# Attention with query/key norm, followed by a gated MLP: score matmuls in clusters of two, weights in eight gated transfers, the gains' load on another queue, and 24 head transposes instead of 14 on TensorE

## The chip, the core and the metric

The kernel runs on one core of one Trainium2 chip. The metric is device microseconds of one execution. Lower is better. A run counts as slow when it is over 1.5% above the fastest run of the same kernel. "TensorE" is PE in the profile, "VectorE" is DVE, "ScalarE" is ACT, "GpSimd" is POOL, "SyncE" is SP.

## The reference, cut to what matters

```python
# q, k, v: (8 batches, 12 heads, 448 tokens, 64), f32; x: (3584, 768); w_in: (768, 2048); w_out: (2048, 768)
q_n, k_n = rmsnorm(q, g_q), rmsnorm(k, g_k)               # over the 64 columns of a head
attn = softmax(q_n @ k_n.T / 8)                            # per head, 448 x 448
x = (attn @ v) -> transposed to (3584 tokens, 768)
h = x @ w_in
g = h * clip(h + 3, 0, 6) / 6
out = g @ w_out                                            # (3584, 768), f32
```

## The kernel before

The work is cut into 48 head pairs (8 batches of 6). A pair is loaded, squared, reduced, scaled to `qks` (bf16), transposed to `kq`, and its keys are multiplied by the product of the two gains `gp` and give `kp`. The scores of a pair come in four steps (`t`), each a matmul for each of the two heads, and each step is followed by an exponential on ScalarE. The values are then gathered, normalised and transposed into `xT`. While one batch is in the attention, the MLP of the batch before it runs between its matmuls on TensorE, with the result `gT` of the first half made by ScalarE and VectorE.

No instruction order is written by hand. Every step is put into a plan with a duration and a due time; a list scheduler on the host orders all steps, and each engine then executes its own in that order. The durations in the plan are guesses. They set an order and nothing else: in the traces below, an instruction starts when its data and its buffers are ready and its engine's earlier instructions are done.

```python
    g_load = add("POOL", 2.5, 0, load_g, xfer=0.1)         # four small loads, issued by GpSimd
    g_make = add("DVE", 0.3, 0, <gp = 8 * gq_t * gk_t>, g_load)
    # ... head pair P
        if P < NPE:                                        # NPE = 7
            # PE transposes of qks into a PSUM buffer of the ring M, then kp and kq by VectorE
        else:
            tr = add("SP", 1.3, at - 5.5, <nc.sync.dma_start_transpose(out=kq, in_=qks)>, ...)
            ks = add("DVE", 0.25, at - 1, <kp = kq[:, 0] * gp>, tr, ...)
    # ... scores
        for t in range(T):
            ps, swar, s_use = S_r.take()                   # S: two PSUM buffers
            s = add("PE", 0.25, at + step * t / T, score, *ks, *swar)     # two matmuls
            x = add("ACT", 0.85, at + step * t / T + 0.2, <e[t] = exp(ps)>, s, *war)
    # ... weights, f32 in memory, bf16 in the core, cast by the transfer
    for c in range(4):
        W_in[c] = add("POOL", 0.9, 12 + 6 * c, lambda c=c: load_w_in(c), xfer=5.3)
    for c in range(8):
        W_out[c] = add("POOL", 0.9, 36 + 3.5 * c, lambda c=c: load_w_out(c), xfer=2.7)
```

Of the kernel before, what the change touches and what calls it, by code (L numbers as in the profile page):

```python
# [20 lines left out]
class Step:  # L21


    __slots__ = ("eng", "dur", "fn", "due", "deps", "xfer", "start", "end", "n")

    def __init__(self, eng, dur, due, fn, deps, xfer=0.0):
        self.eng, self.dur, self.due, self.fn, self.xfer = eng, dur, due, fn, xfer
        self.deps = [d for d in deps if d is not None]
        self.start = self.end = None


class Plan:
# [4 lines left out]
    DMA_LATENCY = 1.7  # L37

# [3 lines left out]
    def add(self, eng, dur, due, fn, *deps, xfer=0.0):  # L42
        s = Step(eng, dur, due, fn, deps, xfer)
        s.n = len(self.steps)
        self.steps.append(s)
        return s

    def order(self):
# [9 lines left out]
        dma_free = 0.0  # L58
# [3 lines left out]
        def release(s):  # L62
            ready[id(s)] = max([0.0] + [
                d.end + (0.06 if d.eng == s.eng and not d.xfer else self.LAT[d.eng]) for d in s.deps])
            open_[s.eng].append(s)
# [5 lines left out]
        while len(done) < len(self.steps):  # L71
# [13 lines left out]
            if s.xfer:  # L85
                dma_free = max(dma_free, s.end) + s.xfer
                s.end = dma_free + self.DMA_LATENCY
# [24 lines left out]
def kernel(  # L112
# [63 lines left out]
    NPE = 7  # L176
    START, FIRST, SECOND, SLOT = 9.0, 4.1, 5.4, 7.9
# [7 lines left out]
    def load_g():  # L185
        for a in range(2):
            nc.gpsimd.dma_start(out=gq_t[a * 64:(a + 1) * 64, :], in_=g_q.rearrange("(p o) -> p o", o=1))
            nc.gpsimd.dma_start(out=gk_t[a * 64:(a + 1) * 64, :], in_=g_k.rearrange("(p o) -> p o", o=1))
# [13 lines left out]
    g_load = add("POOL", 2.5, 0, load_g, xfer=0.1)  # L202
    g_make = add("DVE", 0.3, 0, lambda: nc.vector.scalar_tensor_tensor(
# [10 lines left out]
    def load_w_out(c):  # L214
        nc.gpsimd.dma_start(
            out=w_out_sb[:, 2 * c:2 * c + 2, :],
            in_=moe_w_out[c * 256:(c + 1) * 256, :].rearrange("(f p) n -> p f n", p=128))
# [3 lines left out]
    L, V, KQ = {}, {}, {}  # L221
# [17 lines left out]
    def prep(P):  # L239
# [4 lines left out]
        early = P < 2  # L244
# [13 lines left out]
        else:  # L258
# [3 lines left out]
        red = add("DVE", 1.2, at - 8, lambda: nc.vector.tensor_reduce(  # L262
            out=ssq[0:PT], in_=sq[0:PT].rearrange("p i h (t d) -> p (i h t) d", d=D), axis=AX_X, op=ADD),
            *parts, *war)
        use.append(red)
        rs, war, rs_use = rs_r.take()

        def rstd():
            nc.scalar.activation(out=rs[0:PT], in_=ssq[0:PT], func=LN, bias=D * 1e-6)  # L269
            nc.scalar.activation(out=rs[0:PT], in_=rs[0:PT], func=EXP, scale=-0.5)  # L270

        r = add("ACT", 0.45, at - 7, rstd, red, *war)
        ssq_use.append(r)
        qks, war, qks_use = qks_r.take()
        rs4 = rs[0:PT].rearrange("p (i h t) -> p i h t", i=2, h=2)
        sc = []
        for i in range(2):
            e = "DVE" if P < 2 and i == 0 else "POOL"
            sc.append(add(e, 0.65 if e == "DVE" else 1.1, at - 6, lambda i=i, e=e: (
                nc.vector if e == "DVE" else nc.gpsimd).tensor_tensor(  # L280
                    out=qks[0:PT, i].rearrange("p t h d -> p h t d"),
                    in0=qk[0:PT, i].rearrange("p h (t d) -> p h t d", d=D),
                    in1=rs4[:, i].unsqueeze(3).to_broadcast([PT, 2, T, D]), op=MULT), r, *war))
# [6 lines left out]
        vf_use.append(vc)  # L290
        kq, war, kq_use = kq_r.take()
# [30 lines left out]
    XT, R = {}, {}  # L322

    def attend(P):
# [5 lines left out]
        for t in range(T):  # L330
            ps, swar, s_use = S_r.take()

            def score(t=t, ps=ps):
                for a in range(2):
                    rows = slice(a * 64, a * 64 + 64)
                    nc.tensor.matmul(out=ps[:, a, 0:S], lhsT=kp[rows, t * PT:t * PT + 128],  # L336
                                     rhs=kq[rows, 1, :], start=True, stop=True)

            s = add("PE", 0.25, at + step * t / T, score, *ks, *swar)
            x = add("ACT", 0.85, at + step * t / T + 0.2, lambda t=t, ps=ps: nc.scalar.activation(  # L340
                out=e[0:PT, t], in_=ps[0:PT, :, 0:S], func=EXP), s, *war)
            s_use.append(x)
            exps.append(x)
            kq_use.append(s)
            kp_use.append(s)
        at += step
# [10 lines left out]
        for s in range(NS):  # L357
            av.append(add("PE", 0.31, at + 0.15 * step * s, lambda s=s: values(
# [6 lines left out]
        rest = add("PE", 0.31, at + 0.45 * step, lambda: values(  # L365
# [98 lines left out]
    def y_group(b, i, n, due, span):  # L464
# [4 lines left out]
        for p in range(4):  # L469
            def mm(p=p):  # L470
                for f in range(4 * p, 4 * p + 4):
# [3 lines left out]
                             W_out[2 * p], W_out[2 * p + 1], *war))  # L475
# [27 lines left out]
    def mlp(hb, yb, t0, t1, lead):  # L503
# [17 lines left out]
        for kind, b, what, c in res:  # L521
            due, span = t0 + (t1 - t0) * at / total, (t1 - t0) * c / total
            at += c
            if kind == "h":
                h_group(b, what, due, span)
            else:
                y_group(b, *what, due, span)

    for c in range(4):
        W_in[c] = add("POOL", 0.9, 12 + 6 * c, lambda c=c: load_w_in(c), xfer=5.3)  # L530
    for c in range(8):
        W_out[c] = add("POOL", 0.9, 36 + 3.5 * c, lambda c=c: load_w_out(c), xfer=2.7)

    AHEAD = 5
    for P in range(AHEAD):
        loads(P)
    prep(0)
# [48 lines left out]
```

## Time and profile before

| | before |
|---|---|
| median of the first three runs | 481.65 us (480.47 to 483.04) |
| profiled run, its span | 482.57 us, 480.8 us |
| first scores on TensorE | 16.50 us |
| first w_in matmul on TensorE | 61.85 us |
| TensorE work by spacing (below) | 415.5 us |
| loss (span less that work) | 65.3 us |

The page of the kernel before opens with the span and the busy time of each engine.

```profile
span 480.8 us, 9258 instructions
PE 436.2 (91%) x3658; PEld 237.9 (49%) x3658; DVE 246.6 (51%) x429; ACT 253.3 (53%) x421; POOL 220.9 (46%) x218
```

TensorE is the only engine near its limit. The table by stretches of the kernel before shows where it is and where it isn't; its first row names the columns (start and end of the stretch in us, its length, then busy us of each engine with the number of instructions, the granted TensorE clock, the mean busy share of the DMA engines, and what they moved).

```profile
core 0: us, PE busy (x) PEld busy (x) DVE busy (x) ACT busy (x) POOL busy (x), PEclk, DMA share, GB/s
10.00:48.00 38.00, 24.07 (x220) 14.10 (x220) 21.62 (x37) 18.13 (x29) 20.83 (x23) 0.81 1.17 243
48.00:60.00 12.00, 8.07 (x89) 5.23 (x87) 5.73 (x11) 5.78 (x13) 10.56 (x11) 0.64 1.13 251
60.00:78.00 18.00, 16.72 (x128) 9.59 (x127) 10.59 (x21) 9.80 (x20) 9.37 (x9) 0.98 0.80 177
78.00:100.00 22.00, 18.81 (x196) 10.13 (x195) 14.52 (x24) 17.33 (x30) 20.68 (x17) 1.00 0.73 148
200.00:250.00 50.00, 50.00 (x430) 26.25 (x429) 29.11 (x50) 29.91 (x49) 27.15 (x24) 1.00 0.57 144
```

From 200 to 250 us TensorE is busy in all of the 50 us, so only less TensorE work can shorten that stretch. Before 60 us it is busy in two thirds of the time and at a lower clock, while the DMA share is above 1.1. A share can exceed 1 because the times of packets overlap; no stretch shown here goes above 1.17, so I read 1.1 and more as full. After 60 us the DMA is no longer full in this kernel.

A busy TensorE still hides a cost. The timeline of the kernel before, TensorE alone, has an isolated pair of score matmuls between w_in matmuls (start in us, duration, instruction, shapes, count).

```profile
250.65 0.82 PE L447 MATMUL M<-xT,w_in_sb 128*128 128x512 bf16 x3
251.40 0.36 PE L336 MATMUL S<-kq,kp 64*128 64x448 bf16 x2
251.70 0.82 PE L447 MATMUL M<-xT,w_in_sb 128*128 128x512 bf16 x3
```

Three w_in matmuls of 512 columns and the two score matmuls take 251.70 - 250.65 = 1.05 us together. The three take 0.216 us each in an unbroken sequence, which leaves 0.40 us for the score pair. Where two such pairs stand next to each other, both take 0.59 us. So a pair costs 0.196 us, and each stretch of score matmuls costs about 0.20 us more for going into and out of their shape (64 rows instead of 128). Priced in this way over the built instruction order, TensorE's work is 415.5 us. I call the time at a point less the priced work up to it the loss: it is 42.2 us at the first w_in matmul, 53.5 at 110 us, 58.2 at 159 us, 58.45 at 417 us, and 65.3 at the end.

The start of the kernel before, timeline of VectorE and TensorE (in brackets: idle time of the engine before the instruction, and what ended it):

```profile
9.23 0.16 DVE L203 SCALAR_TENSOR_TENSOR gp<-gq_t,gk_t 128x1 f32<-128x1 f32 x1 [9.23 <-DMA gk_t<-in_g_k_dram]
12.74 0.93 PE L300 MATMUL M<-ident,qks 112*128 112x112 bf16 x8 [12.74 <-DVE qks L280]
16.50 0.93 PE L336 MATMUL S<-kq,kp 64*128 64x448 bf16 x4
39.11 0.55 PE L336 MATMUL S<-kq,kp 64*128 64x448 bf16 x2
61.85 0.34 PE L447 MATMUL M<-xT,w_in_sb 128*128 128x384 bf16 x1
```

VectorE's first instruction is the product of the gains, and it waits 9.23 us for them. The first reduction stands behind it, and the first transposes of TensorE behind that. The isolated score pair at 39.11 us takes 0.55 us; the one at 251.40 above took 0.36. The first w_in matmul starts at 61.85 us. The waits of GpSimd from 15 to 60 us in the kernel before (total us, number of times, longest):

```profile
POOL w_out_sb L215 <- DMA w_in_sb<-in_moe_w_in_dram: 10.6, 3, 5.6
```

GpSimd, which also scales the heads, stands for 10.6 us because the issue of a w_out transfer waits for w_in transfers issued before it.

### The profile page before, as it was taken

To read this page: it belongs to the slowest core of one execution; us is meant where nothing else is said; L and a number is where in the kernel's file an instruction comes from. 1 tells how busy PE (TensorE), PEld (TensorE's weight loads), DVE (VectorE), ACT (ScalarE), POOL (GpSimd) and SP (SyncE) were. 2 spreads that over 40 slices of the span, in tenths; PEclk is the share of its full clock that TensorE was granted. 3 is DMA by queue.
4 is the path that set the end of the run, shared out by engine and by line. 5 is a ranking of instruction groups with operands and counts; after the bars stand their busy time and mean duration, and the time that the engine had idled before them with its cause. 6 is when DMAs were issued, how large, how long until landed. Compare 5 with 4: busy or idle time off the path is not lost.

```text
span 480.8 us, 9258 instructions
## 1 busy us (share of the span) xinstructions
PE 436.2 (91%) x3658; PEld 237.9 (49%) x3658; DVE 246.6 (51%) x429; ACT 253.3 (53%) x421; POOL 220.9 (46%) x218
## 2 busy tenths in 40 slices
PE   0667698968999999999999999999999999999996
PEld 0334454534444555555445565554545555644463
DVE  2636457565877775454566445544444343433421
ACT  3445454885567565656676466655655555322200
POOL 7834866998789853655354634652231000000000
PEclk9985699998999999999999999999999999999999
DMA  7999984999787845766458567562413312211122
GB/s 190 245 245 240 251 183 111 187 194 210 194 231 135 204 102 132 169 169 160 117 132 154 134 148 174 120 172 55 99 29 73 78 49 51 59 34 33 34 64 67
DMA packets 103531, 65.26 MB, mean 136 GB/s; under 512 B 62400, under 2 KB 100032, under 8 KB 103488
## 3 DMA queue, kind: packets, MB, share of 16 engines
q1 hardware_dynamic: 98048, 58.38, 51.5%
q0 software_dynamic: 5440, 6.29, 7.4%
q8 instruction: 28, 0.46, 0.4%
q14 instruction: 15, 0.12, 0.1%
HBM read 45.61 MB, written 11.01 MB: 118 GB/s over the span
## 4 chain that ended last, share of the span: by engine, by line
PE 71%; POOL 10%; issue 8%; DMA 6%; DVE 2%; ACT 2%; POOLq 0%; ACTq 0%
PE M L472 30%; PE M L447 25%; PE S L336 8%; PE X L351 6%; POOL qks L280 4%; DMA w_in_sb<-in_moe_w_in_dram 4%; POOL sq L259 3%; PE R L351 2%; DMA kq<-qks 2%; POOL va L288 1%; DVE gT L455 1%; ACT t L453 1%; ACT e L340 1%; DVE kp L314 1%; POOL sq L251 0%
## 5 line engine op out<-in xcount | busy, mean ns | idle before, releaser
L340 ACT ACTIVATE e<-S 112x896 bf16<-112x896 f32 x192 | 171.4, 915 | 100.6 <-PE S L336 99.3
L447 PE MATMUL M<-xT,w_in_sb 128*128 128x384 bf16 (+1 forms) x768 | 170.5, 354 | 4.4 <-DVE y L480 1.9
L472 PE MATMUL M<-w_out_sb,gT 128*128 128x384 bf16 x896 | 161.6, 326 | 0.7 <-DVE gT L455 0.3
L280 POOL TENSOR_TENSOR qks<-qk,rs 112x512 bf16<-112x512 f32 x94 | 97.6, 1057 | 94.1 <-DMA kq<-qks 60.2
L455 DVE SCALAR_TENSOR_TENSOR gT<-t,M 128x384 bf16<-128x384 f32 (+1 forms) x128 | 79.2, 619 | 82.6 <-ACT t L453 82.3
L453 ACT ACTIVATE t<-M 128x384 f32<-128x384 f32 (+1 forms) x128 | 69.5, 543 | 81.8 <-PE M L447 78.6
L472 PEld LDWEIGHTS <-gT 128*128 128x128 bf16 x896 | 81.3, 98 | 60.1 <-issue 12.6
L447 PEld LDWEIGHTS <-w_in_sb 128*128 128x128 bf16 x768 | 66.8, 97 | 70.0 <-issue 21.1
L259 POOL TENSOR_TENSOR sq<-qk 112x1024 f32<-112x1024 f32 x41 | 78.5, 1919 | 20.1 <-DMA qk<-in_q_dram 13.8
L351 PEld LDWEIGHTS <-e 112*128 112x128 bf16 x1536 | 71.3, 102 | 31.0 <-issue 10.5
L336 PE MATMUL S<-kq,kp 64*128 64x448 bf16 x384 | 71.2, 384 | 11.1 <-ACT e L340 6.4
L480 DVE COPY y<-M 128x384 f32<-128x384 f32 x56 | 31.2, 557 | 70.0 <-PE M L472 70.0
L351 PE MATMUL X<-va,e 112*128 112x65 bf16 x1152 | 61.9, 201 | 1.9 <-ACT e L340 1.5
L262 DVE TENSOR_REDUCE ssq<-sq 112x16 f32<-112x1024 f32 x48 | 58.0, 1212 | 10.5 <-POOL sq L259 10.3
L288 POOL CAST va<-vf 112x512 bf16<-112x512 f32 x48 | 30.2, 630 | 31.7 <-PE R L351 18.1
L336 PEld LDWEIGHTS <-kp 64*128 64x128 bf16 x384 | 18.2, 94 | 51.7 <-issue 41.9
L314 DVE TENSOR_SCALAR kp<-kq,gp 128x448 bf16<-128x448 bf16 x41 | 24.5, 598 | 13.5 <-PE S L336 9.9
L377 DVE TENSOR_TENSOR xn<-X,rd 128x384 bf16<-128x384 f32 x48 | 26.8, 558 | 1.6
L300 PE MATMUL M<-ident,qks 112*128 112x112 bf16 x56 | 6.9, 284 | 21.5 <-DVE qks L280 14.7
L376 DVE RECIPROCAL rd<-X 128x6 f32<-128x6 f32 x48 | 9.3, 194 | 29.1 <-PE X L351 29.0
L351 PE MATMUL R<-va,e 112*128 112x65 bf16 x384 | 21.7, 201 | 0.0
L269 ACT ACTIVATE rs<-ssq 112x16 f32<-112x16 f32 x48 | 10.4, 216 | 12.7 <-POOL qks L280 6.7
(27 smaller groups left out, 69.3 us busy)
## 6 DMA issues: line engine op xcount, KB each, us to landing
qk<-in_k_dram SPq DMA_DIRECT2D x48, 224.0 KB, 3.6
qk<-in_q_dram SPq DMA_DIRECT2D x48, 224.0 KB, 3.9
vf<-in_v_dram SPq DMA_DIRECT2D x48, 224.0 KB, 3.8
w_in_sb<-in_moe_w_in_dram POOLq DMA_DIRECT2D x4, 768.0 KB, 22.1
w_out_sb<-in_moe_w_out_dram POOLq DMA_DIRECT2D x8, 384.0 KB, 28.5
out_dram<-y SPq DMA_DIRECT2D x8, 336.0 KB, 3.2
out_dram<-y SPq DMA_DIRECT2D x8, 288.0 KB, 2.7
out_dram<-y SPq DMA_DIRECT2D x8, 240.0 KB, 2.8
```

Source lines behind the costliest of these rows:

```text
L259: parts.append(add("POOL", 1.95, at - 12, lambda: nc.gpsimd.tensor_tensor(out=sq[0:PT], in0=qk[0:PT], in1=qk[0:PT], op=MULT), *ld, *war))
L262: red = add("DVE", 1.2, at - 8, lambda: nc.vector.tensor_reduce(out=ssq[0:PT], in_=sq[0:PT].rearrange("p i h (t d) -> p (i h t) d", d=D), ...
L280: nc.vector if e == "DVE" else nc.gpsimd).tensor_tensor(
L288: vc = add("POOL", 0.7, at - 3, lambda: nc.gpsimd.tensor_copy(out=va[0:PT, :, :, 0:D], in_=vf[0:PT].rearrange("p h (t d) -> p h t d", d=D) ...
L336: nc.tensor.matmul(out=ps[:, a, 0:S], lhsT=kp[rows, t * PT:t * PT + 128], rhs=kq[rows, 1, :], start=True, stop=True)
L340: x = add("ACT", 0.85, at + step * t / T + 0.2, lambda t=t, ps=ps: nc.scalar.activation(out=e[0:PT, t], in_=ps[0:PT, :, 0:S], func=EXP), s ...
L351: nc.tensor.matmul(out=dst[:, a * E1:(a + 1) * E1], lhsT=e[0:PT, t, a, c0:c0 + 128], rhs=va[0:PT, a, t, :], start=(first and a == 0 and t ...
L447: nc.tensor.matmul(out=m[:, 0:n], lhsT=w_in_sb[:, kt, f * 128:(f + 1) * 128], rhs=X[:, kt, :], start=(kt == 0), stop=(kt == NKT - 1))
L453: r = add("ACT", 0.08 + n / 1200, due + span, lambda: nc.scalar.activation(out=t[:, 0:n], in_=m[:, 0:n], func=RELU, bias=0.5, scale=1.0 / ...
L455: g = add("DVE", 0.12 + n / 960, due + span, lambda: nc.vector.scalar_tensor_tensor(out=G[:, f, :], in0=t[:, 0:n], scalar=1.0, in1=m[:, 0: ...
L472: nc.tensor.matmul(out=m[:, 0:HALF], lhsT=G[:, f, i * 128:(i + 1) * 128], rhs=w_out_sb[:, f, cols], start=(f == 0), stop=(f == NFT - 1))
L480: c = add("DVE", 0.55, due + span, lambda: nc.vector.tensor_copy(out=y[:, cols], in_=m[:, 0:HALF]), *parts, *(ywar if n == 0 else []))
```

## The change

The change means to (1) save half of the shape changes by scoring two steps in a row, which takes both S buffers at once, from the second batch on; (2) keep the DMA transposes of `kq` away from the crowded start: 12 head pairs instead of 7 are transposed by TensorE; (3) start earlier: the gains' loads go to ScalarE's queue, and the first head pair is reduced and scaled in two halves, keys first; (4) keep GpSimd free: eight weight transfers of equal size instead of twelve, each with an earliest time (`after`, the "gate") in the plan; and (5) create the steps in the order of their due times, so that the PSUM buffers of the ring M are handed out in that order.

```diff
-    NPE = 7
-    START, FIRST, SECOND, SLOT = 9.0, 4.1, 5.4, 7.9
+    NPE = 12
+    START, FIRST, SECOND, SLOT = 9.0, 4.1, 5.4, 8.3
...
-            nc.gpsimd.dma_start(out=gq_t[...], in_=g_q...)
-            nc.gpsimd.dma_start(out=gk_t[...], in_=g_k...)
+            nc.scalar.dma_start(out=gq_t[...], in_=g_q...)
+            nc.scalar.dma_start(out=gk_t[...], in_=g_k...)
...
-    g_load = add("POOL", 2.5, 0, load_g, xfer=0.1)
-    g_make = add("DVE", 0.3, 0, ...
+    g_load = add("ACT", 2.2, 0, load_g, xfer=0.1)
+    g_make = add("DVE", 0.1, 7, ...
...
+        for i0, i1 in ([(0, 1), (1, 2)] if P == 0 else [(0, 2)]):      # first head pair: keys, then queries
+            red = add("DVE", 0.6 * n, at - 8 + 0.5 * i0, ...
...
-        for t in range(T):
-            ps, swar, s_use = S_r.take()
+        size = 1 if P < NJ else 2
+        for t0 in range(0, T, size):
+            taken = [S_r.take() for _ in range(size)]
...                                                                    # score(): 2 * size matmuls in a row
+            s = add("PE", 0.2 + 0.196 * size, at + step * t0 / T, score, *ks, *(d for x in taken for d in x[1]))
...
-        W_in[c] = add("POOL", 0.9, 12 + 6 * c, lambda c=c: load_w_in(c), xfer=5.3)
-        W_out[c] = add("POOL", 0.9, 36 + 3.5 * c, lambda c=c: load_w_out(c), xfer=2.7)
+    def weights(c, at, load, kept):
+        kept[c] = add("POOL", 0.9, at, lambda: load(c), *(L[1][2] if at < 8 else []), xfer=4.4, after=at)
...
+        blocks.append((0.0, lambda c=c: weights(c, 7.0 + 6.0 * c, load_w_in, W_in)))
+        blocks.append((0.0, lambda c=c: weights(c, 33.0 + 6.0 * c, load_w_out, W_out)))
+    ...                                                                # all blocks, sorted by due time, then run
```

Cut here: the plan's model of how software transfers and hardware transfers share the DMA (it only changes the order), the split of `prep` and `attend` into two parts each, the squares of the third head pair (all on ScalarE now, as for the first two), and small changes of durations. In the built order, the stretches of score matmuls fall from 155 to 102, and TensorE's transposes of `qks` grow from 56 to 96.

## The prediction

> **What bounds it now.** From about 110 us on, TensorE: the table by stretches shows PE 100% busy from 200 to 420 us. I price PE's work by its spacing in the timeline: w_in matmul 0.216 us at 512 columns and 0.163 at 384, w_out matmul 0.163, a value set of eight 0.266, an isolated score pair 0.40. Two adjacent score pairs take 0.59, not 0.80, so each change into and out of the score shape costs about 0.20. The Trainium skill ("TensorEngine Tiling (Array Packing)", Key Properties) says that changing the tiling mode drains TensorE; the spacing agrees. Over the built instruction order this gives 415.5 us of PE work. Two middle batches (159.4 to 262.7 us) sum to 103.1 and took 103.3, so the prices hold. The other 65 of the 480.8 us are losses: 42 before the first w_in matmul at 61.85 us (seven head pairs scored, 20 us of work), 11 from there to 110 us, 5 to 159 us, 2 in the tail, 4.4 after the last matmul.
>
> The first loss has these sources in the timeline. PE starts at 12.74 us because DVE's first reduction waits until 9.2 us behind the g product; its squares were ready at 4.9. GpSimd waits 1.9, 5.6 and 3.1 us (22 to 38 us) to issue w_out transfers behind earlier w_in ones, which holds up head scaling. DMA is saturated (about 245 GB/s) to 57 us. PE runs slow till 54 us (value set 0.57 us).
>
> **What the change does.**
> 1. Clusters. In the built order, stretches of score matmuls fall from 155 to 102, not by half, since some were adjacent already: 53 x 0.20 = -10.6 us of PE. A cluster takes both S buffers, so it can wait for two exponentials (2 x 0.92): I allow +2 us in the middle.
> 2. Forty more PE transposes at about 0.065: +2.6 us. PE work becomes 407.5 us. Five DMA transposes of kq go, and with them PE waits of 1.2 to 1.4 us for kp at 82, 103 and 107 us.
> 3. g on ScalarE's queue, and the first head reduced k, then q: first scores near 10.5 us instead of 16.5.
> 4. Eight software transfers, placed between GpSimd's head work: the three waits go (10.6 us), and head loads meet fewer weight bytes early. The bytes stay.
> 5. M banks in due order: a little of the 11 us.
>
> **Sum.** The seven heads before the first w_in matmul are then limited by slow-clock PE, about 4.9 us a head (the rate at 16 to 30 us before), so that matmul starts near 43 us, a loss of 22 instead of 42. Then 5 instead of 11, 2 instead of 5, 2 new in the middle, 2 in the tail, 4.4 at the end: 407.5 + 37 = 445; I shade to **443 us**, range 432 to 457, about 8% faster. Nearly all of it is on the critical path, since PE sets the time after the start. Faster by over 2%: 0.96; same 0.03; slower 0.01.
>
> **What would show it.** First transposes near 8 us; no GpSimd idle released by w_in transfers; first w_in matmul near 43 us; two middle batches in about 99.7 us instead of 103.3; PE waits for e in the middle under 2 us; tail unchanged at 64 us.
>
> **What would make it wrong.** The weights still take half of the DMA and starve the heads, so the first w_in matmul stays after 50 us; the slow clock lasting longer; PE waiting at each cluster for exponentials (0.3 us x 72 = 20 us would eat much of the gain); or everything fitting better, PE near its floor of 407.5 + 20.

## The result, and the profile after

| | before | after |
|---|---|---|
| median (four runs each, the first profile's three among those before) | 482.16 us | 462.24 us (459.64 to 464.77) |
| ratio | | 0.9591 (95%: 0.952 to 0.9661) |
| profiled run, its span | 482.57, 480.8 us | 459.64, 457.8 us |
| first scores | 16.50 us | 14.44 us |
| first w_in matmul | 61.85 us | 48.02 us |
| priced TensorE work | 415.5 us | 407.5 us |
| loss | 65.3 us | 50.3 us |

A ratio here is the mean time of one kernel's fast runs over the mean of the other's fast runs of the same rounds, so it is not quite the ratio of the medians quoted beside it. The kernel is 4.1% faster. The prediction had 443 us and a range up to 457; the measured time lies outside.

The page of the changed kernel:

```profile
span 457.8 us, 9354 instructions
PE 418.9 (92%) x3698; PEld 229.7 (50%) x3698; DVE 252.3 (55%) x434; ACT 249.1 (54%) x425; POOL 212.3 (46%) x209
```

TensorE is busy for 17.3 us less, with 40 more instructions. The table by stretches of the changed kernel, same columns as before:

```profile
10.00:48.00 38.00, 27.19 (x322) 16.42 (x322) 30.62 (x52) 27.23 (x50) 30.49 (x33) 1.00 1.15 262
48.00:60.00 12.00, 9.03 (x91) 5.17 (x89) 7.03 (x14) 7.77 (x15) 12.00 (x12) 1.00 1.17 226
60.00:78.00 18.00, 17.18 (x213) 10.53 (x212) 13.72 (x27) 14.88 (x28) 17.84 (x18) 1.00 1.13 216
78.00:100.00 22.00, 16.11 (x153) 8.07 (x150) 12.71 (x22) 10.17 (x20) 14.84 (x14) 0.84 1.11 224
```

Two things stand out. The start is much denser (322 TensorE instructions instead of 220 before 48 us). And the DMA stays full for longer: its share is 1.13 and 1.11 after 60 us, where it was 0.80 and 0.73. From 78 to 100 us TensorE is busy for less time than in the kernel before (16.11 against 18.81 us), at a lower clock. (The same times hold different work in the two kernels, so this is a symptom and no account.)

The marks of TensorE in the changed kernel's timeline:

```profile
48.02 2.12 PE L485 MATMUL M<-xT,w_in_sb 128*128 128x384 bf16 x12
102.61 2.77 PE L510 MATMUL M<-w_out_sb,gT 128*128 128x384 bf16 x16
242.04 0.55 PE L368 MATMUL S<-kq,kp 64*128 64x448 bf16 x4
243.57 3.41 PE L510 MATMUL M<-w_out_sb,gT 128*128 128x384 bf16 x20
344.00 3.41 PE L510 MATMUL M<-w_out_sb,gT 128*128 128x384 bf16 x20
```

The x4 at 242.04 is a cluster (two steps, four matmuls). Between the two bursts of twenty w_out matmuls, 243.57 and 344.00, two middle batches pass in 100.4 us; 99.7 had been predicted, and they took 103.3 before. The loss at these marks is 27.3 us at 48.02, 40.2 at 102.61, 42.3 at 243.57, 43.0 at 344.00, and 50.3 at the end of the span. So the gain of 23.0 us in the span is 8.0 us of TensorE work and 15.0 us of loss, and the loss falls only before the first w_in matmul (42.2 to 27.3). The stretch that follows it loses 12.9 us to the burst of sixteen w_out matmuls at 102.61. The like burst of the kernel before comes at 115.38 us, with about 12.8 us lost since 61.85, so this stretch is no better than before. (The mark at 110.48, with 11.3 us, is the first w_in matmul of 512 columns; in the changed kernel that one comes at 98.39, with about 11.8 us lost since 48.02.)

About half of what the start gained is TensorE working faster. Up to the first w_in matmul it is busy for 33.7 us with 19.7 us of priced work in the kernel before, and for 27.2 us with 20.7 us of it in the changed one; the other half is less idle time. The record of the granted clock shows half speed from 33.5 to 54.0 us before, and full speed from 32.5 to 83.7 us in the changed kernel, where an isolated score pair takes:

```profile
33.19 0.36 PE L368 MATMUL S<-kq,kp 64*128 64x448 bf16 x2
```

That is 0.36 us against the 0.55 at 39.11 us before. (For the time before 32.5 us the changed kernel's trace has no record of the clock, and the table puts 1.00; the pair at 31.41 us still takes 0.56.)

The start of the changed kernel, timeline of GpSimd, VectorE and TensorE:

```profile
1.67 1.01 POOL L233 DMA_DIRECT2D w_in_sb<-in_moe_w_in_dram  x1
10.03 0.16 DVE L226 SCALAR_TENSOR_TENSOR gp<-gq_t,gk_t 128x1 f32<-128x1 f32 x1 [10.03 <-DMA gk_t<-in_g_k_dram]
12.05 0.55 PE L330 MATMUL M<-ident,qks 112*128 112x112 bf16 x4 [12.05 <-DVE qks L305]
14.44 0.93 PE L368 MATMUL S<-kq,kp 64*128 64x448 bf16 x4 [0.84 <-DVE kq L336]
```

The gains are now issued by ScalarE, and VectorE waits longer for them (10.03 us instead of 9.23). The Trainium skill says why another issuing engine need not help ("DMA: Bandwidth & Descriptors", "Issuing engines are not separate DMA queues"): transfers from all of these engines run on the same 16 DMA engines and interleave, and issuing from another engine saves only the issue time. The trace agrees: the gains' four loads took 3.0 to 7.3 us from issue to landing, against 4.5 to 6.1 before. The first line shows one competitor: the first w_in transfer goes out at 1.67 us, though the plan's gate said 7.0. The gate and the dependency on the second head's loads exist in the plan only. Nothing on the chip holds the transfer back, and no head work stands before it in GpSimd's order.

The place of the largest single wait later on, timeline of the changed kernel (SPq is SyncE's queue of issues):

```profile
77.59 1.70 SPq L341 DMA_TRANSPOSE kq<-qks  x1
83.38 0.34 DVE L344 TENSOR_SCALAR kp<-kq,gp 128x448 bf16<-128x448 bf16 x1 [5.11 <-DMA kq<-qks]
84.76 0.55 DVE L493 SCALAR_TENSOR_TENSOR gT<-t,M 128x384 bf16<-128x384 f32 x1
85.36 2.08 PE L485 MATMUL M<-xT,w_in_sb 128*128 128x384 bf16 x6 [5.09 <-DVE gT L493]
```

This is the first head pair (the thirteenth) whose keys and queries still go through a DMA transpose. It is issued at 77.59 us and lands 5.8 us later. VectorE stands at `kp` for 5.11 us, the next `gT` stands behind it, and TensorE waits 5.09 us for the M buffer that this `gT` would give back. The Trainium skill ("TensorE: Matmul & The Clock Gate", "Engine queue depths" under "Architectural detail") calls ScalarE and VectorE strict FIFO; the trace agrees, as no VectorE instruction runs in those 5.11 us. The clock falls to half at 83.7 us, while TensorE waits, and stays there until 90.5 us (0.84 over the stretch from 78 to 100 us).

### The profile page after: what moved, and what is told of

It reads as the page before. It is cut to its first block, busy times and chain, and to the rows that moved or that the text cites. A ratio compares the mean times of both kernels' runs of the same rounds, so it can differ in the third digit from the quotient of the medians.

```text
span 457.8 us, 9354 instructions
## 1 busy us (share of the span) xinstructions
PE 418.9 (92%) x3698; PEld 229.7 (50%) x3698; DVE 252.3 (55%) x434; ACT 249.1 (54%) x425; POOL 212.3 (46%) x209
## 2 busy tenths in 40 slices
DMA packets 99020, 64.13 MB, mean 140 GB/s; under 512 B 57888, under 2 KB 95520, under 8 KB 98976
## 4 chain that ended last, share of the span: by engine, by line
PE 74%; DMA 8%; DVE 6%; ACT 4%; POOL 3%; issue 2%; SPq 1%; ACTq 0%; POOLq 0%; DVEq 0%
PE M L510 31%; PE M L485 25%; PE S L368 8%; PE X L389 7%; DMA qk<-in_q_dram 4%; DVE gT L493 3%; ACT e L373 3%; DMA kq<-qks 2%; PE R L389 2%; DVE ssq L290 2%; POOL sq L282 2%; ACT t L491 2%; DMA qk<-in_k_dram 2%; POOL qks L305 1%; DMA xT<-xr 1%
## 5 line engine op out<-in xcount | busy, mean ns | idle before, releaser
L373 ACT ACTIVATE e<-S 112x896 bf16<-112x896 f32 x192 | 166.5, 914 | 49.2 <-PE S L368 49.0
L510 PE MATMUL M<-w_out_sb,gT 128*128 128x384 bf16 x896 | 159.0, 327 | 1.9 <-DVE gT L493 1.4
L305 POOL TENSOR_TENSOR qks<-qk,rs 112x512 bf16<-112x512 f32 x94 | 96.5, 1046 | 75.8 <-DMA kq<-qks 55.7
L510 PEld LDWEIGHTS <-gT 128*128 128x128 bf16 x896 | 83.7, 98 | 63.4 <-issue 13.0
L282 POOL TENSOR_TENSOR sq<-qk 112x1024 f32<-112x1024 f32 x41 | 77.6, 1894 | 15.2 <-DMA qk<-in_q_dram 11.5
L389 PEld LDWEIGHTS <-e 112*128 112x128 bf16 x1536 | 64.8, 99 | 28.9 <-issue 14.0
L290 DVE TENSOR_REDUCE ssq<-sq 112x16 f32<-112x1024 f32 (+1 forms) x49 | 58.2, 1190 | 7.0 <-POOL sq L282 6.4
L368 PE MATMUL S<-kq,kp 64*128 64x448 bf16 x384 | 57.4, 369 | 3.2 <-ACT e L373 1.3
L389 PE MATMUL X<-va,e 112*128 112x65 bf16 x1152 | 56.7, 196 | 0.5 <-ACT e L373 0.4
L344 DVE TENSOR_SCALAR kp<-kq,gp 128x448 bf16<-128x448 bf16 x36 | 27.3, 759 | 15.1 <-PE S L368 8.0
L368 PEld LDWEIGHTS <-kp 64*128 64x128 bf16 x384 | 12.5, 95 | 31.9 <-issue 27.0
L296 ACT ACTIVATE rs<-ssq 112x16 f32<-112x16 f32 (+1 forms) x49 | 10.5, 215 | 28.3 <-DVE ssq L290 15.1
L414 DVE RECIPROCAL rd<-X 128x6 f32<-128x6 f32 x48 | 9.2, 193 | 19.3 <-PE X L389 19.2
```

The lines of the kernel that those rows point to most:

```text
L282: parts.append(add("POOL", 1.95, at - 12, lambda: nc.gpsimd.tensor_tensor(out=sq[0:PT], in0=qk[0:PT], in1=qk[0:PT], op=MULT), *ld, *war))
L290: red = add("DVE", 0.6 * n, at - 8 + 0.5 * i0, lambda i0=i0, i1=i1, cs=cs: nc.vector.tensor_reduce(out=ssq[0:PT, cs], in_=sq[0:PT, i0:i1]. ...
L305: nc.vector if e == "DVE" else nc.gpsimd).tensor_tensor(
L368: nc.tensor.matmul(out=ps[:, a, 0:S], lhsT=kp[rows, c0:c0 + 128], rhs=kq[rows, 1, :], start=True, stop=True)
L373: x = add("ACT", 0.93, at + step * (t0 + i) / T + 0.2, lambda t=t0 + i, ps=ps: nc.scalar.activation(out=e[0:PT, t], in_=ps[0:PT, :, 0:S], ...
L389: nc.tensor.matmul(out=dst[:, a * E1:(a + 1) * E1], lhsT=e[0:PT, t, a, c0:c0 + 128], rhs=va[0:PT, a, t, :], start=(first and a == 0 and t ...
```

## The experiments

The theories had the following names in the expectations, in short. For the late start, A: VectorE's order (the product of the gains stands ahead of the reductions); B: the first weight transfer takes the DMA from the gains and the first heads. For the wait at 80 us, C (and C1): VectorE's order (`kp` ahead of `gT`); D: GpSimd has no time left, so that `qks` comes late; E: the DMA is full, because the weights are read at the same time, and the transpose lands late; E2: it is the DMA transposes of batch 1's values that fill it; F: SyncE's order of issue. Each call to the chip had its own runs of the kernel before (medians 482.05 to 482.76 us), and its ratio is the fair comparison across calls. All kernels of the experiments ran in up to six timed executions. Where I give a difference in us, it is one of medians; worked out from the ratios, the differences from the changed kernel come out between 0.4 and 2.3 us lower.

An edit that *moves* a step takes it out of the finished order and puts it back elsewhere; in the built order nothing else moved. An edit of a number of the plan (`NPE`, `size`, a ring) lets the list scheduler run again, so that other steps move as well. That is a weakness of these runs.

### The changed kernel again

> The changed kernel itself, unchanged, timed beside the next three on the same chip. Expected ratio to the kernel before 0.955 to 0.965, and its single runs may spread over some 5 us as its first four did (459.6 to 464.8 us).

Measured: 461.66 us (460.33 to 465.0), ratio 0.9596 (0.9565 to 0.9627). The differences below are against this run. Its profile has the same wait near 80 us, but longer:

```profile
86.73 2.08 PE L485 MATMUL M<-xT,w_in_sb 128*128 128x384 bf16 x6 [6.64 <-DVE gT L493]
```

The first w_in matmul comes at 47.84 us and the burst of sixteen at 103.54, 55.7 us later (54.6 in the first profile). So two profiles of one kernel differ by 1.5 us in this wait and by 1.1 us in this stretch. Each kernel below was profiled once, and differences of this size in it show nothing.

### The start: the gains' product later, the first weight transfer later, both

```diff
# product later (a move)
+    move_after(g_make, <the second transpose of head pair 0>)      # just before the first kp
# transfer later (a move)
+    move_after(W_in[0], <the cast of v of head pair 1>)
```

> Only the g product moves in VectorE's order, from ahead of the first reductions to just ahead of the first kp. Theory A (g alone holds the start): first scores 4 us earlier (near 10.5 us instead of 14.4) and the total 3 to 4 us lower. Theory B (the first weight transfer holds it, and g is only one of the things that land late): the next reduction in VectorE's order waits for the second head's q, which landed near 11.7 us, so the first scores come less than 1 us earlier and the total moves less than 1.5 us.

> Only the first w_in transfer moves in GpSimd's order, from its first place (issued at 1.7 us) to behind the second head's v cast (near 16 us). Theory B: g lands by about 6 us instead of 10, the second head's q by about 7 us instead of 11.7, first scores near 10 us, total 3 to 5 us lower. Theory A: g still lands near 9 to 10 us because its own descriptors are slow, first scores within 1 us of 14.4, total the same. A third view (the pace of the later heads is set elsewhere) expects the earlier first scores but less than 1 us in the total.

> Both moves together. Theory B: nearly the same as the weight move alone, at most 1 us better. Theory A: the gain of the g move alone. If the first scores come before 10 us and the total falls by less than 1 us, the start was not on the critical path at all.

Measured: product later 460.27 us, 0.9548 (0.9521 to 0.9574); transfer later 459.52 us, 0.953 (0.9503 to 0.9557); both 460.1 us, 0.9536 (0.9502 to 0.9569). The timeline of the run with the product later:

```profile
8.06 0.56 PE L330 MATMUL M<-ident,qks 112*128 112x112 bf16 x4 [8.06 <-DVE qks L305]
11.84 1.22 DVE L290 TENSOR_REDUCE ssq<-sq 112x16 f32<-112x1024 f32 x1 [3.84 <-ACT sq L272]
14.04 0.93 PE L369 MATMUL S<-kq,kp 64*128 64x448 bf16 x4 [4.54 <-DVE kq L336]
```

The transposes start near 8 us, as I had predicted of the change itself, but then the second head pair's reduction waits for that pair's late queries, the first `kp` comes behind it, and the first scores come at 14.04 instead of 14.44. The first w_in matmul stays at 48.29. A is a wait that another hides. The timeline of the run with the transfer later:

```profile
6.26 0.16 DVE L226 SCALAR_TENSOR_TENSOR gp<-gq_t,gk_t 128x1 f32<-128x1 f32 x1 [6.26 <-DMA gk_t<-in_g_k_dram]
8.28 0.56 PE L331 MATMUL M<-ident,qks 112*128 112x112 bf16 x4 [8.28 <-DVE qks L305]
10.67 0.93 PE L369 MATMUL S<-kq,kp 64*128 64x448 bf16 x4 [0.84 <-DVE kq L337]
43.85 2.12 PE L486 MATMUL M<-xT,w_in_sb 128*128 128x384 bf16 x12
```

With one transfer issued at 10.47 us instead of 1.67, the product comes at 6.26, the transposes at 8.28, the scores at 10.67, and the first w_in matmul at 43.85: the prediction's 8, 10.5 and 43. B holds. But the time falls by only 2.1 us (3.2 by the ratios). The burst of sixteen w_out matmuls comes at 100.73 us, 1.9 us earlier than in the first profile of the changed kernel and 2.8 us earlier than in its repeat, so 30 to 55% of what was gained at the start is given back there. The wait at 80 us is 7.2 us; against 5.1 and 6.6 in the two profiles of the changed kernel, that it grew is not shown. Both moves together give no more (first w_in matmul at 44.90, longest wait 6.3 us).

### The wait at 80 us: VectorE's order, fewer DMA transposes early, GpSimd's load

```diff
# kp of the 13th pair three VectorE steps later (a move)
+    move_after(KP[12], dve[dve.index(KP[12]) + 3])
# two more head pairs transposed by TensorE (re-planned)
-    NPE = 12
+    NPE = 14
# casts of v of pairs 6 to 14 on ScalarE (only ScalarE's and GpSimd's instructions changed)
-    vc = add("POOL", 0.7, at - 3, lambda: nc.gpsimd.tensor_copy(
+    vc = add("POOL", 0.7, at - 3, lambda: (nc.scalar.copy if 5 <= P < 14 else nc.gpsimd.tensor_copy)(
# NPE = 14 together with the first weight transfer later
```

> Only one VectorE instruction moves: kp of the 13th head pair (the first whose keys are transposed by DMA) goes behind the next gate product instead of ahead of it. In the changed kernel VectorE stood 5.1 us at this instruction, and TensorE behind it. Theory C1 (VectorE's order made the stall): the wait near 80 us shrinks under 1 us, total 5 to 7 us lower. Theory C2 (the DMA transpose itself is late, and the scores of that head are next in TensorE's order anyway): TensorE then waits 3 to 4 us at these scores instead, total at most 2 us lower.

> The PE transposes two more head pairs (14 instead of 12), so the first DMA transposes of keys come after the last transposes of batch 1 on the same queue. Theory C2: no TensorE wait over 2 us between 75 and 90 us, no slow clock after it, total 5 to 8 us lower in spite of 1 us more PE work. Theory D (GpSimd, busy without a gap from 36 to 83 us, sets the pace of this stage): the wait moves but stays, total within 2 us of the changed kernel.

> The v casts of head pairs 6 to 14 run on ScalarE instead of GpSimd (0.6 us each, 5.4 us taken off GpSimd between 36 and 83 us), all else in its order. Theory D: total 3 to 5 us lower. Theory C2: within 1.5 us of the changed kernel, since the first DMA transpose of keys stands behind the transposes of batch 1 in its queue, whenever GpSimd is done.

> The weight move of the earlier run together with 14 head pairs transposed by the PE. If the start and the stall near 80 us are the two steps that the prediction missed, both gains come in full: first w_in matmul near 44 us, the stretch from there to the w_out burst of sixteen (102.6 us in the changed kernel) shorter by 6 to 8 us, total 449 to 453 us. If GpSimd or the DMA sets the pace of this stage, at most 3 us below the weight move alone.

Measured: `kp` moved 462.16 us (461.55 without its one slow run), 0.9566 (0.9515 to 0.9616); `NPE = 14` 461.72 us (460.77 without its two slow runs), 0.953 (0.9474 to 0.9585); casts on ScalarE 460.13 us, 0.9535 (0.9495 to 0.9575); `NPE = 14` with the later transfer 458.36 us, 0.9493 (0.9452 to 0.9534). The timeline of the run with `kp` moved:

```profile
84.62 0.34 DVE L344 TENSOR_SCALAR kp<-kq,gp 128x448 bf16<-128x448 bf16 x1 [4.08 <-DMA kq<-qks]
88.44 2.08 PE L511 MATMUL M<-w_out_sb,gT 128*128 128x384 bf16 x6 [6.91 <-DVE gT L494]
```

Three steps of VectorE did run ahead of `kp`, but `kp` still waits, later `gT` steps stand behind it and behind the next `kp`, and TensorE waits 6.91 us. C1 falls: the order only says who stands first. With `NPE = 14` the wait splits in three (1.9, 2.5 and 2.7 us), and VectorE waits 5.17 us at the first pair that still uses the DMA, now the fifteenth. With 5.4 us less work on GpSimd (the casts on ScalarE), the wait is 6.6 us, no shorter than in the two profiles of the changed kernel; D falls as its cause. That kernel was 1.5 us faster by the medians, with intervals that overlap, and I don't explain that. `NPE = 14` with the later transfer had been expected at 449 to 453 us if the start and this wait were the two steps that the prediction missed: the first w_in matmul came at 41.89 us, but waits of up to 2.7 us remained, and the median is only 1.2 us below the later transfer alone.

### The wait at 80 us: no w_out transfers, and the transposes of the keys issued first

The first of the two **computes a wrong result**: w_out is set to zero by VectorE, and its four transfers are left out. All other work is there.

```diff
# no w_out transfers
+    nc.vector.memset(w_out_sb[:], 0.0)
     def load_w_out(c):
-        nc.gpsimd.dma_start(out=w_out_sb[...], in_=moe_w_out[...])
+        pass
# SyncE's order (a move): the key transposes of pairs 13 and 14 ahead of the xT/xr transposes just before them
+    for P in (12, 13):
+        while <the issue just before kq's of P is an xT or xr transpose>:
+            move_after(<that issue>, <kq's of P>)
```

> A wrong result on purpose: w_out is set to zero by VectorE at the start and none of its four transfers is issued; every other engine keeps its order, TensorE does the same matmuls. This takes 3.1 MB of weights out of the DMA traffic between 46 and 76 us, and 3.2 us of issue work off GpSimd. Theory E (the DMA is full in this stage, so that the critical transposes and loads land late): DMA share falls clearly below 1.1 between 45 and 75 us, the wait of 5.1 us near 80 us shrinks under 1.5 us, total 5 to 9 us lower. Theory F (the order in SyncE's queue and in VectorE, not the bytes): the wait near 80 us stays over 3 us, total within 3 us.

> Only SyncE's order changes: the DMA transposes of the keys of head pairs 13 and 14 go ahead of the transposes of batch 1 next to them (xn of one pair, xr of three). Theory F: the first transpose of keys is issued near 75 us instead of 77.6, lands near 79 to 80 instead of 83.3, the TensorE wait of 5.1 us shrinks under 2.5 us, total 3 to 5 us lower. Theory E: the landing stays after 82 us although the issue is earlier, total within 1.5 us.

Measured: without w_out transfers 453.39 us (452.54 to 454.13), 0.9407 (0.9388 to 0.9426), 8.3 us less than the changed kernel (9.1 by the ratios); keys issued first 461.36 us, 0.9581 (0.9551 to 0.9611). The table by stretches of the run without w_out transfers:

```profile
60.00:78.00 18.00, 17.18 (x219) 10.66 (x217) 13.81 (x28) 14.85 (x30) 16.15 (x16) 1.00 0.70 180
78.00:100.00 22.00, 19.87 (x169) 10.21 (x169) 14.15 (x26) 14.45 (x27) 22.00 (x20) 1.00 0.92 210
```

The share of the DMA falls from 1.13 to 0.70 and from 1.11 to 0.92, and the clock stays at 1.00. Its timeline has the same transpose (the first of keys by DMA), the same `kp`, and the burst of sixteen:

```profile
70.24 1.25 SPq L341 DMA_TRANSPOSE kq<-qks  x1
77.09 0.62 DVE L344 TENSOR_SCALAR kp<-kq,gp 128x448 bf16<-128x448 bf16 x1
95.23 2.77 PE L510 MATMUL M<-w_out_sb,gT 128*128 128x384 bf16 x16
```

The transpose is issued 7.4 us earlier and lands 3.0 us after its issue (5.8 in the changed kernel); `kp` comes long after that, with no wait. TensorE's longest wait in the stretch is now 2.0 us, and the burst of sixteen comes at 95.23 us instead of 102.61, from a w_in matmul at 48.5. So the stretch took 46.7 us instead of 54.6 (55.7 in the repeat), 7.9 to 9.0 us less: TensorE is idle for 4.5 us of it instead of 9.8, and most of the rest is that its clock does not fall. E holds in its first part: with w_out not read in this time, most of the loss is gone. (GpSimd loses 3.2 us of issue work as well, but taking 5.4 us off it left the wait as it was.)

E says that the transpose lands late after its issue. That is the smaller part: in the changed kernel it lands 10.2 us later than without w_out's transfers, and 7.4 us of that lie before its issue, in SyncE's queue. The timeline of the changed kernel has there:

```profile
63.37 5.60 SPq L438 DMA_TRANSPOSE xT<-xn  x1
```

This one issue holds SyncE for 5.60 us, where the like issue took 1.20 us without w_out's transfers, and all later ones stand behind it. Why it takes so long, and whether that is itself an effect of the full DMA, is not shown. The timeline of the run with the keys' transposes issued first:

```profile
74.48 3.63 SPq L341 DMA_TRANSPOSE kq<-qks  x1
83.72 0.34 DVE L344 TENSOR_SCALAR kp<-kq,gp 128x448 bf16<-128x448 bf16 x1 [6.33 <-DMA kq<-qks]
```

Issued 3.1 us earlier than in the changed kernel, it lands at about the same time, 9.2 us after its issue, and VectorE waits 6.33 us. F falls: an earlier place in the queue buys nothing here. (SyncE had been held for 6.15 us by an issue at 63.86 us in this run too.)

### No clusters, and seven pairs on TensorE as before

```diff
# no clusters (re-planned)
-        size = 1 if P < NJ else 2
+        size = 1
# seven pairs (re-planned)
-    NPE = 12
+    NPE = 7
```

> Single score pairs everywhere (the rest of the change stays). The built order has 172 stretches of score matmuls instead of 102: at 0.20 us each 14 us more PE work. The prediction's price says 472 to 477 us; two middle batches in 103.9 us instead of 100.4. If clusters cost as much in waits for both S buffers as they save, the total stays within 4 us.

> Seven head pairs transposed by the PE as before the change, instead of twelve; the rest of the change stays. PE work falls by 2.7 us. The prediction's claim (five DMA transposes fewer take their kp waits away) says the total rises by 2 to 6 us, with kp waits between 55 and 85 us. If the DMA transposes only move the stall from the 13th head pair to the 8th, the total stays within 2 us.

Measured: no clusters 476.43 us, 0.9881 (0.9861 to 0.9901); seven pairs 474.92 us, 0.9846 (0.9815 to 0.9878). The built order without clusters has 172 stretches of score matmuls instead of 102. Seventy stretches at 0.20 us are 14.0 us, and the kernel is 14.8 us slower than with clusters (13.7 by the ratios), so the price holds; of the difference, re-planning may have a part. Two middle batches took 106.1 us, more than the 103.9 expected: by the prices they are 104.1, with 45 stretches of score matmuls, and one wait of 2.1 us for another buffer comes on top. The waits of TensorE between 45 and 115 us with seven pairs:

```profile
PE S L368 <- DVE kp L344: 17.0, 3, 8.9
```

Five pairs back on the DMA cost 13.3 us (12.0 by the ratios). The first w_in matmul stays at 48.36 us, so the cost lies after it. Three waits of 17.0 us in total stand at `kp`, and the DMA transposes of the keys land up to 19.9 us after their issue. I had expected 2 to 6 us: the prediction had valued this part of the change by the waits of 1.2 to 1.4 us in the kernel before, where the DMA was no longer full after 60 us. In the changed kernel the same transposes would meet a full one.

### Rings of four, batch 1's values transposed by TensorE, the old weight transfers, a combination

```diff
# rings of four: fewer loads can run ahead (re-planned)
-    qk_r = Ring(tiles("qk", 6, [128, 2, 2, T * D], FP32))
-    vf_r = Ring(tiles("vf", 5, [128, 2, T * D], FP32))
+    qk_r = Ring(tiles("qk", 4, [128, 2, 2, T * D], FP32))
+    vf_r = Ring(tiles("vf", 4, [128, 2, T * D], FP32))
# batch 1's values (re-planned)
-        if b == 0:                     # transposes of xn by TensorE, out=xT[0]
+        if b < 2:                      # ... out=xT[b]
# old transfers: four of w_in, eight of w_out, no "after", as in the kernel before (re-planned)
# combination: first weight transfer later, NPE = 18, batch 1's values by TensorE
```

> Four buffers for q and k and four for v instead of six and five, so loads run at most four head pairs ahead. Theory E1 (the loads that run ahead fill the DMA and delay what is needed at once): by the stall near 80 us some 1.3 to 1.4 MB less has been asked for, which is 5 to 6 us of a full DMA at 240 GB/s; the wait near 80 us shrinks under 2 us, total 3 to 6 us lower. If shorter prefetch only makes GpSimd wait for loads, the total rises by 2 to 6 us.

> The six transposes of normalized values of batch 1 go to the PE (18 more matmuls, 1.1 us of PE, six copies of 0.36 us on VectorE) instead of the DMA. Theory E2 (the small-packet transposes are what fills the DMA): the wait near 80 us shrinks under 2.5 us and the wait for the xr transpose near 100 us stays, total 2 to 5 us lower. If only the bytes of loads and weights count, the total is within 1.5 us.

> The twelve ungated weight transfers of the kernel before in the changed kernel. The prediction gave their gating most of the 20 us by which it expected the first w_in matmul earlier: first w_in matmul 8 to 12 us later (56 to 60 us), GpSimd waits of some 10 us at w_out transfers. By theory E the bytes are the same, and what is lost at the start comes back in the stage from 48 to 103 us, where then fewer weights are under way: total only 1 to 5 us higher. By the prediction's reading, 8 to 12 us higher.

> A candidate: first w_in transfer behind the second head's v cast, 18 head pairs and the values of batch 1 transposed by the PE. PE work 4.2 us above the changed kernel. If theory E holds, no DMA transpose of keys falls into the full stage: no TensorE wait over 2 us between 60 and 100 us, the stretch from the first w_in matmul to the burst of sixteen under 52 us, total 450 to 456 us. If not, 458 to 463 us.

Measured: rings of four **455.94 us** (454.94 to 456.25), 0.9446 (0.9426 to 0.9466); batch 1's values by TensorE 464.41 us, 0.9624 (0.9602 to 0.9646); old transfers 468.23 us (467.17 to 470.17), 0.971 (0.9683 to 0.9736); combination 460.93 us, 0.9553 (0.9534 to 0.9572).

The table by stretches of the run with rings of four, and then its timeline:

```profile
78.00:100.00 22.00, 19.20 (x179) 10.18 (x176) 13.35 (x22) 13.48 (x24) 19.36 (x18) 0.92 0.94 202
```

```profile
74.11 2.14 SPq L341 DMA_TRANSPOSE kq<-qks  x1
80.72 0.40 DVE L344 TENSOR_SCALAR kp<-kq,gp 128x448 bf16<-128x448 bf16 x1 [2.86 <-DMA kq<-qks]
```

`kp` waits 2.86 us instead of 5.11, TensorE's longest wait is 2.7 us, and the share of the DMA from 78 to 100 us is 0.94 instead of 1.11. The first w_in matmul is at 48.08 as before, and the burst of sixteen comes at 97.2 instead of 102.61 us. The idea was that loads of later pairs, issued as soon as a buffer is free, take the DMA from transposes that are needed now. It is only partly supported: by 77.6 us one query load less had been issued (17 instead of 18), and the first four transposes of keys landed in 5.6 us in the median (4.5 in the changed kernel), so no sooner; the plan was also made anew. But the first of them was issued at 74.11 us instead of 77.59, and no issue of a DMA transpose took over 2.8 us on SyncE, as without w_out's transfers. That the version is faster is measured; why SyncE is not held up in it is not settled.

With batch 1's values on TensorE the wait at 80 us is still 5.2 us, so E2 falls. The kernel is 2.8 us slower by the medians and 1.3 by the ratios, with intervals that overlap: that it is slower at all is not shown.

With the old transfers the first w_in matmul comes at 63.59 us, 15.6 us later than with the new ones, and GpSimd waits 15.7 us (10 to 45 us) for w_in transfers at the issue of the w_out ones. So the new transfers, with their places in GpSimd's order, are what brought the start forward. (Part of the 15.6 us is the clock, whose record shows full speed for the first time at 52.3 us here, and at 32.5 with the new transfers.) But the kernel is only 6.6 us slower, and one reason is that from there to the burst of sixteen it takes 48.8 us instead of 54.6 (5.8 us back). That lies between the 1 to 5 us of theory E and the 8 to 12 of the prediction's reading. The start and the next stretch share one supply: bytes that don't hold up the one hold up the other.

The combination speaks against a simple E, by which it should have run in 450 to 456 us. No DMA transpose of keys falls into the full stage (the first is issued at 118.5 us), and TensorE has no wait over 1.5 us from 60 to 100 us, but from the first w_in matmul to the first one of 512 columns it still loses about 10.9 us (11.8 in the changed kernel), in many short waits for `gT`. So the late transposes of keys are one way in which this stretch loses time, and not the only one.

### The rings of four with the later first transfer

```diff
# rings of four + first weight transfer later; the second kernel: NPE = 14 as well
```

> The shorter prefetch (four buffers each) together with the moved first w_in transfer; only that one GpSimd instruction differs from the run with four buffers. If the two steps that were missed are separate, their gains add: 5.7 + 2.1 us, total 453 to 455 us, first w_in matmul near 44 us. If both act on the same full DMA, the total stays at 455 to 457 us.

> The same with 14 head pairs transposed by the PE. If a late DMA transpose of keys still costs (the run with four buffers kept a wait of 2.7 us near there), total 1 to 3 us below the run without it; if not, up to 1 us above it (1.1 us more PE work).

Measured: 455.88 us (454.99 to 459.76), 0.946 (0.9425 to 0.9495); with `NPE = 14` 457.04 us, 0.9473 (0.944 to 0.9505). The gains don't add up. In the first kernel the first scores come at 11.49 us, but the first w_in matmul comes at 48.26, not near 44: GpSimd waits 7.4 us for `rs`, and the clock falls to 0.66 and 0.50 between 30 and 50 us. The wait alone does not account for it: the kernel with `NPE = 14` has one of 7.7 us, but its clock stays at 1.00 there, and its first w_in matmul comes at 43.77 (it then loses 5.1 us in one wait at 75.6 us).

From its first w_in matmul the first kernel needs 45.7 us to the burst of sixteen, as short as without w_out's transfers, though w_out is read and the share of the DMA is 1.25 from 60 to 78 us. Its first transpose of keys is issued at 70.44 us and `kp` does not wait. So a full DMA alone does not make this stretch long. Its lead of 3.3 us over the rings of four alone at the burst is gone at the end (spans of 454.3 and 454.4 us); where it goes is not settled.

The fastest versions found are the rings of four with and without the later transfer (0.946 and 0.9446, not told apart). With rings of four alone the kernel is 5.5% faster than the kernel before and 1.2% faster than the changed one by the medians, 1.6% by the ratios.

## Why the prediction was wrong

The direction and most of the mechanisms held. The time did not: 462.24 us against 443, and above the range's end of 457. Two steps of the sum failed: the start ("a loss of 22 instead of 42", measured 27.3) and, above all, "Then 5 instead of 11" for the stretch after it (measured 11.8 to 12.9). The prediction summed 407.5 us of TensorE work and 37.4 us of loss and shaded the 445 to 443. The 19.2 us that it missed split as follows (loss measured in the profiled run less loss predicted, by the marks above):

| term | predicted | measured | missed by |
|---|---|---|---|
| TensorE work, priced | 407.5 | 407.5 (same order, same prices) | 0 |
| loss before the first w_in matmul | 22 | 27.3 | 5.3 |
| loss from there to 102.61 us | 5 | 12.9 | 7.9 |
| loss in the middle (2 + 2) | 4 | 3.1 | -0.9 |
| tail and end (2 + 4.4) | 6.4 | 7.0 | 0.6 |
| shading of the sum | -1.9 | | 1.9 |
| time of the run less its span, not added | 0 | 1.8 | 1.8 |
| profiled run to the median | 0 | 2.6 | 2.6 |

The mark at 102.61 is not quite the one that the prediction meant. Its 5 us end at the first w_in matmul of 512 columns (110.48 before, 98.39 after); measured there, the second term is about 11.8 us, missed by 6.8, and the third takes up the difference.

**Right: the clusters.** "stretches of score matmuls fall from 155 to 102 ... 53 x 0.20 = -10.6 us of PE". The two middle batches took 100.4 us where 99.7 was predicted, TensorE's waits there were 0.7 us in total and none of them for `e`, and taking the clusters away cost 13.7 to 14.8 us where 14.0 is the price of seventy stretches. So the measured size of the drain that the prediction named is 0.20 us for going in and coming back.

**Right: GpSimd and the tail.** The waits of GpSimd for w_in transfers went from 10.6 us to none between 15 and 60 us, and the run with the old transfers brought them back (15.7 us) together with a start 15.6 us later. The last batch took 64.2 us where "tail unchanged at 64 us" was predicted.

**Wrong: the first step of the start.** "g on ScalarE's queue ... first scores near 10.5 us instead of 16.5" and "head loads meet fewer weight bytes early". The first weight transfer was issued earlier (1.67 instead of 4.40 us) and not later, as the gate is no wait on the chip. The gains came no sooner, and the scores began at 14.44. Postponing this one transfer gave 8.28, 10.67 and 43.85 us for the three marks that the prediction had at 8, 10.5 and 43. So the 5.3 us of the first term come from this step. That the rest of the start fitted was partly luck. The prediction's pace of 4.9 us a head was that of a slow clock; the pace was met (33.6 us from the first scores to the first w_in matmul, 33.2 with the transfer later, 32.5 predicted), although TensorE ran at full clock from 32.5 us (27.7 with the transfer later) and stood idle for over 7 of these 33 us. What set the pace instead is not shown. I could have seen it in the built order, where that transfer stands ahead of all head work of GpSimd.

**Wrong: the second term, "Then 5 instead of 11".** This is the largest. I reasoned that M buffers in due order and five DMA transposes fewer would take away most of the waits after the start. They did take away those waits. But w_out's transfers, which the change issues from 46.3 to 62.0 us instead of 7.7 to 37.6, plus the head loads that now follow faster (18 query loads issued by 78 us instead of 15), fill the DMA until 100 us instead of 60. In that time SyncE's issues were held up, the first DMA transpose of keys was issued at 77.59 us and landed 5.8 us later, VectorE and then TensorE stood behind it for 5.1 us, and the clock fell to half for 6.8 us. So this term measured 11.8 to 12.9 us instead of 5. Leaving out w_out's transfers took the stretch from 54.6 to 46.7 us. That this is just the 7.9 us of the table is partly chance (6.8 at the prediction's own mark; 9.0 us saved against the repeat). I had written "The bytes stay" and had not followed the bytes into the next stretch.

**Wrong: the size of the extra TensorE transposes.** The prediction set +2.6 us of work against waits of 1.2 to 1.4 us at three places. In the changed kernel those five pairs are worth 12.0 to 13.3 us, since without them the transposes land up to 19.9 us after their issue. This error worked the other way: without this gain, which lies after the first w_in matmul, the second term would have been missed by more.

**Not settled.** What exactly fills the DMA beside w_out; why an issue on SyncE can take 5.60 us, and why it does not with rings of four; what made the combination lose as much in the stretch without late keys; what sets the pace of the start; and why the granted clock falls around 80 to 90 us. The wait of 5 us begins before that, but no run took the wait alone away at the same DMA traffic.

## What to carry to other kernels

When transfers are moved out of a crowded start, follow their bytes: they arrive in the next stretch, and one small transfer that is late there, in front of an engine that works in order, can cost a good part of what was gained. A time in a host-side plan orders instructions and holds none of them back, so look in the built order for what stands first on the engine that issues. Price shape changes on TensorE by the spacing of matmuls, not by busy time: of all terms of this prediction, that one held.

## What the Trainium skill lacked or had wrong

- "TensorEngine Tiling (Array Packing)", Key Properties: it states the drain at a change of mode and gives no cost. Here going into 64-row score matmuls and back costs about 0.20 us a stretch (0.40 us for an isolated pair against 0.59 us for two adjacent ones; seventy stretches more made the kernel 13.7 to 14.8 us slower).
- "TensorE: Matmul & The Clock Gate", Back-to-back issue gap: it gives about 131 ns as the sustained spacing of matmuls with 512 columns in a real kernel, and N/2.4 + 2.5 ns (216 ns) as the isolated gap. Here the sustained spacing is 0.216 us at 512 columns, and 128 w_out matmuls of 384 columns took 20.96 us, 0.164 us each. The formula fits sustained work; the smaller figure does not.
- "DMA: Bandwidth & Descriptors", Specifications and Latency and other measured facts: it gives limits of 435 and about 358 GB/s, and a memory latency of up to 2 us at high load, but not how long a small transfer on the critical path takes when the DMA is full. Here the share was 1.11 to 1.17 at 216 to 262 GB/s (95,520 of the changed kernel's 99,020 packets are under 2 KB), and DMA transposes of one head pair, the first of which landed 3.0 us after its issue where w_out was not being read, took 5.8, 9.2 and up to 19.9 us. Nor does it give a figure for how long an issue can hold its engine then: one issue of a DMA transpose took 5.60 us on SyncE, 1.20 without w_out's transfers.
- No page says that an earliest time in a scheduling plan is not a wait on the chip; here a transfer with a gate at 7.0 us went out at 1.67 us, and the first scores came 3.8 us later than with it moved (14.44 against 10.67).
